# Two weight conversions per unit at the start of a group, four units without one, and three smaller moves, in a fused chunk attention and feed-forward kernel

## The chip, the cores and the metric

The kernel runs on one core of one Trainium2 chip. The metric is device time in microseconds for one execution, the median of three runs before the change.

## What is computed

Attention in chunks of 64 rows over eight heads of width 64, and then a feed-forward layer without a residual:

```python
scores = scale * np.matmul(q_c, k_c.transpose(0, 1, 2, 4, 3))
scores = scores - np.max(scores, axis=-1, keepdims=True)
attn = np.exp(scores)
attn = attn / (np.sum(attn, axis=-1, keepdims=True) + 1e-09)
out = np.matmul(attn, v_c)
...
h = x @ w_in
g = h - np.tanh(h)
return (g @ w_out).astype(np.float32)
```

Here x is the attention's output, 4608 tokens of 512 values, w_in is 512 by 2048 and w_out 2048 by 512, all float32 at the interface.

## The kernel before the change

The 4608 tokens are 36 pairs of 128, in nine groups of four pairs (512 tokens). Each product is made of two halves: a value is split into a high part and the rest, and of the four partial products three are computed.

**Group 0** uses weights as loaded (two float32 tiles, `wh` and `wl`), **group 1** float16 halves of w_in and the float32 halves of w_out, **groups 2 to 8** (class `Fast`) float16 throughout, with sums of w_out blocks that spare one multiplication in eight. While group 0 runs, the attention of groups 0 and 1 (class `Early`, pairs 0 to 7) runs too. While group 1 runs, the weights are converted for it and for what follows, and the attention of group 2 (class `Late`) runs.

**A unit** is one block of 128 columns of w_in. A group has 16 units, in group 1 in the order of `ORDER`; below u0 to u15. For each unit, `FeedForward.written` does in this order: `split` of the unit before (ScalarE rounds it to `gh`, VectorE subtracts to `gl`), the extra steps filed in `at` under 2s-0.5, `gemm1` (12 matmuls into one of two PSUM tiles `ph`), `shrink` (ScalarE tanh into `t`, VectorE h minus tanh), the steps under 2s, `gemm2` of an earlier unit (12 matmuls), and the steps under 2s+1. Every engine takes its instructions in the order in which they are written. So `gemm1` of unit s needs the `ph` of unit s-2 to be free, which in group 1 is after that unit's `gl` (line 554).

**A conversion** (`Half.convert`, lines 448 to 458; below c0 to c15, one per unit, needed by that unit's `gemm1`) is two ScalarE instructions (lines 454 and 455: the two float16 parts) and two of VectorE (457: what the first rounding left; 458: add it to the second part). c(i) writes its parts over the low half of the unit before in `ORDER` (`convert(i)`, line 971), and the same memory is where c(i-1) keeps the intermediate of its line 457, read last by its line 458. So the first ScalarE instruction of c(i) may start only after line 458 of c(i-1). c0, c1 and c2 are made at the end of group 0, c3 to c15 are filed in `at`, c(i) in unit i-3.

**The group's scales.** `ahead` files the steps of `Late`: `greatest` (VectorE makes the scales `to` and `exp` in unit 3, from a maximum that goes out to memory and back), `split` of q, k and v (ScalarE 340, VectorE 341), scores, softmax, transposes, values. `power_of` is six VectorE instructions over one column.

**Pair 6.** `PLAN` is the written order of group 0. Its token `n6` sums pair 6's exponents and divides by the sums head by head, eight ScalarE instructions (line 235). `N` does it with one VectorE instruction (line 237).

Of the kernel before, what the change touches and what calls it, by code (L numbers as in the profile page):

```python
# [18 lines left out]
ALU = mybir.AluOpType  # L19
# [4 lines left out]
H = 8  # L24
# [7 lines left out]
FC = DFF // P  # L32
# [6 lines left out]
FAST = 2  # L39
FAST_LAG = 2  # L40
AHEAD = 3
RAW = 3
WS = 2
EARLY_FC = 8
# [5 lines left out]
ORDER = tuple(i // 2 + i % 2 * FC // 2 for i in range(FC))  # L50

PLAN = """
l0.0 A0 A1 l1.0 v0 v1 a2 a3 l0.1 v2 v3 l1.1 l2.0 l2.1 a4 a5 l3.0 l3.1 F15 x0.0 b0.0 i0.0 z0.0 W0.0 S0 S1 q0 x1.0 m0 p0 e1 P1 F13 S2 N0 T0 b1.0 i1.0 S3 N1 x0.1 z1.0 W1.0 T1 F2 m2 p2 e3 U2 V0 F3 G0.0 D2 P3.0 P3.1 b0.1 U3 D3 i0.1 t T2 x1.1 b1.1 G1.0 t T3 s i1.1 z0.1 W0.1 F2 V2 s z1.1 W1.1 H Y G0.1 x2 G1.1 b2 t s i2 t x3 z2.0 w2.0 s z2.1 w2.1 H h S4 S5 b3 i3 | l4.0 l4.1 v4 v5 z3.0 w3.0 z3.1 w3.1 M4 g2 h l5.0 l5.1 c4 M5 g3 h N4 N5 T4 T5 V4 a6 a7 l6.0 l6.1 c5 S6 S7 v6 v7 g4 h E6 l7.0 l7.1 c6 g5 h M7 l8.0 l8.1 c7 g6 h n6 N7 T6 T7 V6 Z c8 g7 h l9.0 l9.1 c9 g8 h l10.0 l10.1 c10 g9 h l11.0 l11.1 c11 g10 h X l12.0 l12.1 c12 g11 h l13.0 l13.1 c13 g12 h l14.0 l14.1 c14 g13 h l15.0 l15.1 c15 g14 h g15 h h
"""

@with_exitstack
def attn_ffn_kernel(ctx: ExitStack, tc: tile.TileContext, qE, kE, vE, qL, kL, vL, w_in, w_out, out):
# [8 lines left out]
    nc = tc.nc  # L66
# [20 lines left out]
    def place_of(a, part, fc, dtype=F16):  # L87

        return w_pool[fc].tile([P, DM], F32R, name=f"w{a}{part}{fc}").bitcast(dtype)
# [6 lines left out]
    def new_x():  # L96
        return tuple(xpool.tile([P, KC, MOST], F32R, name=f"x{a}") for a in "hl")

    def new_half_x():

        t = xpool.tile([P, KC, MOST], F32R, name="xh").bitcast(F16)
        return t[:, :, :MOST], t[:, :, MOST:]
# [17 lines left out]
    def load_weights(pool, fc, part):  # L120
        if part == 0:
            raws[fc] = pool.tile([P, 2, DM, 2], U32, name="raw", bufs=RAW)
        nc.sync.dma_start(out=raws[fc][:, part], in_=(w_in, w_out)[part][fc])
# [284 lines left out]
    class Half:  # L408
# [39 lines left out]
        def convert(self, fc, place):  # L448


            half_w[fc] = place.rearrange("p (a n) -> p a n", a=2)
            (h, l), (h16, l16), to = wt[fc][0], (half_w[fc][:, i] for i in range(2)), self.to[:, 0:1]
            h, l = h.bitcast(F32), l.bitcast(F32)
            nc.scalar.activation(h16, h, AF.Copy, scale=to)
            nc.scalar.activation(l16, l, AF.Copy, scale=to)
            rest = place_of("l", 0, fc)[:, :DM]
            nc.vector.scalar_tensor_tensor(out=rest, in0=h, scalar=to, in1=h16, op0=ALU.mult, op1=ALU.subtract)  # L457
            nc.vector.tensor_add(l16, l16, rest)
# [57 lines left out]
    class FeedForward:  # L516
# [21 lines left out]
        def shrink(self):  # L538
            fc, t0, t1, n, ph = self.ph
            t = ffn.tile([P, MOST], F32, name="t", bufs=3)[:, :n]  # L540
            if self.g:
                nc.scalar.activation(t, ph, AF.Tanh, scale=self.sig)
                nc.vector.scalar_tensor_tensor(out=ph, in0=ph, scalar=self.sig, in1=t, op0=ALU.mult, op1=ALU.subtract)  # L543
            else:
                nc.scalar.activation(t, ph, AF.Tanh)
                nc.vector.tensor_sub(t, ph, t)
            self.ready = fc, t0, t1, n, ph if self.g else t

        def split(self):
            fc, t0, t1, n, t = self.ready  # L550
# [214 lines left out]
    def ahead(att, at, g):  # L765

        o = 2 * FC * (g - FAST)

        def put(unit, part, f, *args):
            at[o + 2 * unit + part].append(lambda: f(*args))  # L770

        late = g == FAST
        later = g == FAST + 1
        put(1 + later, 0, sums, att, g, "q")
        if not late:
            put(2 + later, 0, sums, att, g, "k")
            put(0 if later else -3, later, att.halves, g, 0)
            put(2, not later, att.halves, g, 1)
        put(1 if late else 4, late, att.sent, g)
        put(2 if late else 4, not late, att.returned, g)  # L780
        put(3 if late else 5, 1, att.greatest, g)
        put(9, 1, lambda: powers.update({g: half.power_of(g)}))
        put(6, 0, lambda: xs.update({g: new_half_x()}))
        for b, u in enumerate((3, 13) if late else (6, 14)):
            put(u, 1, att.split, g, b, "q")
            put(u + 1, 0, att.split, g, b, "k")
            other = u + 2 if late and b else u + 1
            put(other, 1, att.split, g, b, "v")
            if g + 1 < NG:
                for i in (2 * b, 2 * b + 1):  # L790
                    put(u + 1, 1, att.load, FIRST[g + 1] + i, i, "qk")
                    put(other, 1, att.load, FIRST[g + 1] + i, i, "v")
            u += late
            put(u + 2, 0, att.scores, g, b)
            put(u + 2, 1, att.shifted, g, b)
            put(u + 3, 0, att.exponent, g, b)
            put(u + 3, 1, att.totals, g, b)
            put(u + 4, 0, att.divided, g, b)
            put(u + 4 + (not (late and b)), late and b, att.transpose, g, b)
            at[o + 2 * u + 17 - late].insert(0, lambda b=b: att.values(g, b, xs[g]))  # L800
# [4 lines left out]
    x, x1 = new_x(), xpool.tile([P, KC, MOST], F32R, name="xl").bitcast(F32)  # L805
# [13 lines left out]
    att = Early(pool, [psum, ps_a], 4)  # L819
# [28 lines left out]
    def step(token):  # L848
# [53 lines left out]
        elif kind == "q":  # L902
            square(n, 0, junk)
        elif kind == "z":
            high(n, part)
        elif kind in "wW":
            low(n, part, nc.gpsimd if kind == "W" else None)
        elif kind in "Gg":
            gemm1(n, part)
            if kind == "g":  # L910
                shrink()
                split()
        elif kind == "t":
            shrink()
        elif kind == "s":
            split()
        elif kind == "H":
            ff.gemm2((((0, 0),), ((1, 0),), ((0, 1),)))
        elif kind == "h":
            ff.gemm2()  # L920
        elif kind == "Y":
            first_psum.close()
            att.psum = [ps_a]
            ps_o2 = ctx.enter_context(tc.tile_pool(name="ps_o2", bufs=1, space=PSUM, reuse_waits="tile"))
            ff.room(ps_o2, range(2, 4))
            pools.append(ps_o2)
        elif kind == "Z":
            first.close()
            late = ctx.enter_context(tc.tile_pool(name="late_weights", bufs=1, reuse_waits="tile"))
            weight_tiles(late, range(EARLY_FC, FC))  # L930
# [18 lines left out]
    late = ctx.enter_context(tc.tile_pool(name="att", bufs=1, side="right", reuse_waits="tile"))  # L949
    w_pool.update((fc, late) for fc in SPARE)  # L950
    att, half = Late(late), Half(late)
# [4 lines left out]
    xs, powers, at, made = {}, {}, defaultdict(list), {}  # L956
# [13 lines left out]
    def convert(i):  # L970
        half.convert(ORDER[i], place_of("l", 0, ORDER[i - 1]) if i else first_place)

    for i in range(AHEAD, FC):
        at[2 * (i - AHEAD) - 0.5].append(lambda i=i: convert(i))
    at[6].append(for_attention)
    for g in range(FAST, NG):
        ahead(att, at, g)
# [19 lines left out]
    with tc.manual_schedule():  # L997
        half.most(0)
        half.powers(0)
        half.scale_of_sum()  # L1000
        for i in range(AHEAD):
            convert(i)
# [67 lines left out]
```

## Time and profile before

| what | us |
|---|---|
| median of 3 runs | 796.07 (795.02 to 796.33) |
| the profiled execution, device time | 794.97 |
| its span, first to last instruction | 793.2 |
| TensorE busy | 781.5 (99%) |
| VectorE busy | 630.7 (80%) |
| ScalarE busy | 466.8 (59%) |
| GpSimd busy | 407.9 (51%) |

The span is shorter than the device time of the same execution by 1.8 us, which lie around it. Busy times of different engines overlap. All times in the rows further below are in us from the start of the span. Line numbers are those of the kernel before; in the changed kernel the same statements stand one or two lines lower.

### The profile page before, as it was taken

To read this page: it belongs to the slowest core of one execution; us is meant where nothing else is said; L and a number is where in the kernel's file an instruction comes from. 1 tells how busy PE (TensorE), PEld (TensorE's weight loads), DVE (VectorE), ACT (ScalarE), POOL (GpSimd) and SP (SyncE) were. 2 spreads that over 40 slices of the span, in tenths; PEclk is the share of its full clock that TensorE was granted. 3 is DMA by queue.
4 is the path that set the end of the run, shared out by engine and by line. 5 is a ranking of instruction groups with operands and counts; after the bars stand their busy time and mean duration, and the time that the engine had idled before them with its cause. 6 is when DMAs were issued, how large, how long until landed. Compare 5 with 4: busy or idle time off the path is not lost.

```text
span 793.2 us, 21231 instructions
## 1 busy us (share of the span) xinstructions
PE 781.5 (99%) x9096; PEld 659.0 (83%) x9099; DVE 630.7 (80%) x856; ACT 466.8 (59%) x714; POOL 407.9 (51%) x461
## 2 busy tenths in 40 slices
PE   8999999999999999999999999999999999999997
PEld 4877885656788888888888888888888888888887
DVE  5897987999799887877878687968796878687554
ACT  6888996766486446545654474546454655454332
POOL 1100003477786656564656556656656465656463
PEclk9999999999999999999999999999999999999999
DMA  9854442210232322231313123222322230302000
GB/s 355 323 181 156 156 160 63 81 25 8 77 91 81 55 81 55 61 84 34 89 42 97 35 89 57 69 55 81 65 81 55 82 64 2 55 2 54 2 27 27
DMA packets 61054, 64.62 MB, mean 81 GB/s; under 512 B 33952, under 2 KB 42016, under 8 KB 60960
## 3 DMA queue, kind: packets, MB, share of 16 engines
q1 hardware_dynamic: 60528, 62.61, 27.3%
q8 instruction: 71, 1.16, 0.6%
q10 hardware_dynamic: 432, 0.66, 0.2%
q14 instruction: 23, 0.19, 0.1%
HBM read 46.47 MB, written 9.45 MB: 70 GB/s over the span
## 4 chain that ended last, share of the span: by engine, by line
PE 86%; DVE 7%; ACT 4%; issue 1%; DMA 0%; POOL 0%; POOLq 0%; ACTq 0%; DVEq 0%; SPq 0%
PE ph L616 37%; PE po L656 31%; PE po L564 6%; PE ph L534 6%; PE psa L352 3%; DVE wl L457 1%; PE po L731 1%; DVE ph L543 1%; PE ph L863 1%; DVE gl L554 1%; ACT s L217 1%; ACT gh L553 1%; PE psa L182 1%; DVE wh L503 1%; ACT w L132 0%
## 5 line engine op out<-in xcount | busy, mean ns | idle before, releaser
L616 PE MATMUL ph<-xh,wl 128*128 128x256 f16 x2520 | 291.1, 273 | 0.0
L616 PEld LDWEIGHTS <-wl 128*128 128x128 f16 x2520 | 245.4, 98 | 29.3 <-issue 0.5
L625 POOL TENSOR_TENSOR xl<-xl 128x256 f32<-128x256 f32 x111 | 111.8, 1008 | 222.6 <-DVE xl L624 222.0
L623 ACT ACTIVATE t<-ph,sig 128x512 f32<-128x512 f32 x112 | 77.0, 687 | 216.2 <-PE ph L616 214.6
L624 DVE SCALAR_TENSOR_TENSOR xl<-ph,sig,t 128x512 f32<-128x512 f32 x112 | 83.5, 745 | 78.7 <-ACT t L623 78.6
L656 PEld LDWEIGHTS <-wh 128*128 128x128 f16 x1134 | 110.9, 98 | 12.9
L627 POOL TENSOR_TENSOR xl<-xl 128x256 f32<-128x256 f32 x111 | 103.9, 936 | 0.0
L626 POOL TENSOR_TENSOR xl<-xl 128x128 f32<-128x128 f32 x111 | 102.2, 921 | 0.0
L656 PE MATMUL po<-wl,wh 128*128 128x256 f16 x648 | 101.0, 273 | 0.0
L637 DVE SCALAR_TENSOR_TENSOR gl<-xl,to_g,gh 128x896 f16<-128x896 f32 x56 | 83.4, 1489 | 8.0 <-ACT gh L636 8.0
L656 PE MATMUL po<-wh,wh 128*128 128x256 f16 x486 | 85.5, 273 | 0.0
L637 DVE SCALAR_TENSOR_TENSOR wh<-xl,to_g,wh 128x896 f16<-128x896 f32 x56 | 71.1, 1269 | 16.6 <-ACT wh L636 14.8
L656 PEld LDWEIGHTS <-gh 128*128 128x128 f16 x756 | 73.0, 98 | 8.8
L636 ACT ACTIVATE wh<-xl,to_g 128x896 f16<-128x896 f32 x56 | 57.9, 1035 | 32.4 <-POOL xl L627 31.5
L534 PE MATMUL ph<-xh,wl 128*128 128x512 f16 (+2 forms) x252 | 59.5, 376 | 2.5 <-DVE gl L554 2.4
L656 PE MATMUL po<-wh,gh 128*128 128x256 f16 x380 | 61.5, 273 | 0.0
L656 PE MATMUL po<-wl,gh 128*128 128x256 f16 x376 | 58.7, 273 | 0.0
L636 ACT ACTIVATE gh<-xl,to_g 128x896 f16<-128x896 f32 x56 | 57.8, 1032 | 1.3 <-DVE from L114 0.6
L564 PE MATMUL po<-wh,gh 128*128 128x512 f32 x128 | 52.8, 415 | 0.0
L564 PE MATMUL po<-wl,gh 128*128 128x512 f32 x128 | 50.1, 394 | 0.2 <-POOL wl L147 0.2
L656 PEld LDWEIGHTS <-gl 128*128 128x128 f16 x378 | 37.0, 98 | 4.3
L656 PE MATMUL po<-wh,gl 128*128 128x256 f16 x190 | 39.2, 273 | 0.0
(176 smaller groups left out, 1245.7 us busy)
## 6 DMA issues: line engine op xcount, KB each, us to landing
raw<-w_in SPq DMA_DIRECT2D x16, 512.0 KB, 4.0
raw<-w_out SPq DMA_DIRECT2D x16, 512.0 KB, 5.5
xl<-qL SPq DMA_DIRECT2D x28, 256.0 KB, 3.0
rawk<-kL SPq DMA_DIRECT2D x28, 256.0 KB, 3.3
rawv<-vL SPq DMA_DIRECT2D x28, 256.0 KB, 3.4
out<-wh SPq DMA_DIRECT2D x55, 128.0 KB, 1.8
q<-qE SPq DMA_DIRECT2D x8, 256.0 KB, 5.9
v<-vE SPq DMA_DIRECT2D x8, 256.0 KB, 6.1
```

What stands on the lines that cost most here:

```text
L352: nc.tensor.matmul(ps(c, e, hp)[u * D:(u + 1) * D], lhsT=stationary(a, r, e, hp, u), rhs=moving(b, r, e, hp, u), start=first, stop=(i == 2 ...
L534: nc.tensor.matmul(ph, lhsT=w[:, kc * P:(kc + 1) * P], rhs=x[b][:, kc, cols], start=(k == 0), stop=(k == 3 * KC - 1))
L564: nc.tensor.matmul(self.po[t], lhsT=gg[a][:, ts], rhs=wt[fc][1][b], start=(fc == 0 and a == b == 0), stop=(fc == FC - 1 and a == 1))
L616: nc.tensor.matmul(self.ph[:, 1 - f::2, :], lhsT=half_w[fc][:, w, kc * P:(kc + 1) * P], rhs=rhs, start=(k == 0), stop=(k == 3 * KC - 1))
L623: nc.scalar.activation(t, self.ph, AF.Tanh, scale=sig)
L624: nc.vector.scalar_tensor_tensor(out=u[:, :4], in0=self.ph, scalar=sig, in1=t, op0=ALU.mult, op1=ALU.subtract)
L625: engine.tensor_add(u[:, 4:6], u[:, 1:3], u[:, 0:4:3])
L626: engine.tensor_add(u[:, 6], u[:, 1], u[:, 2])
L627: engine.tensor_sub(u[:, 0:4:3], u[:, 0:2], u[:, 2:4])
L636: nc.scalar.activation(gh, u, AF.Copy, scale=powers[1])
L637: nc.vector.scalar_tensor_tensor(out=gl, in0=u, scalar=powers[1], in1=gh, op0=ALU.mult, op1=ALU.subtract)
L656: nc.tensor.matmul(place[m], lhsT=part[:, self.SUM[m]], rhs=w[m][:, o], start=first, stop=(last and part is gl), skip_group_check=True)
```

## The change

In `PLAN`, the token `n6` becomes `N6` (the line is long and otherwise the same). The rest:

```diff
@@ -39,6 +39,7 @@
+CONVERTED = (0, 0, 1, 1, 2, 2, 3, 5, 6, 7, 11, 12, 13)
...
@@ -538,13 +539,14 @@
         def shrink(self):
             fc, t0, t1, n, ph = self.ph
             t = ffn.tile([P, MOST], F32, name="t", bufs=3)[:, :n]
+            u = ph if self.g and fc else t
             if self.g:
                 nc.scalar.activation(t, ph, AF.Tanh, scale=self.sig)
-                nc.vector.scalar_tensor_tensor(out=ph, in0=ph, scalar=self.sig, in1=t, op0=ALU.mult, op1=ALU.subtract)
+                nc.vector.scalar_tensor_tensor(out=u, in0=ph, scalar=self.sig, in1=t, op0=ALU.mult, op1=ALU.subtract)
             else:
                 nc.scalar.activation(t, ph, AF.Tanh)
-                nc.vector.tensor_sub(t, ph, t)
-            self.ready = fc, t0, t1, n, ph if self.g else t
+                nc.vector.tensor_sub(u, ph, t)
+            self.ready = fc, t0, t1, n, u
...
@@ -779,10 +781,10 @@
-        put(9, 1, lambda: powers.update({g: half.power_of(g)}))
+        put(14 if late else 9, 1, lambda: powers.update({g: half.power_of(g)}))
         put(6, 0, lambda: xs.update({g: new_half_x()}))
         for b, u in enumerate((3, 13) if late else (6, 14)):
-            put(u, 1, att.split, g, b, "q")
+            put(u + late, -0.5 if late else 1, att.split, g, b, "q")
...
@@ -970,8 +972,8 @@
-    for i in range(AHEAD, FC):
-        at[2 * (i - AHEAD) - 0.5].append(lambda i=i: convert(i))
+    for i, slot in enumerate(CONVERTED, AHEAD):
+        at[2 * slot - 0.5].append(lambda i=i: convert(i))
```

Conversions c3 to c15 stood one in each of units 0 to 12. They now stand two each in units 0, 1 and 2 (c3 to c8), one each in units 3, 5, 6, 7, 11, 12 and 13, and none in units 4, 8, 9 and 10. `late` is true for the third group (group 2) alone: its `power_of` goes from unit 9 to unit 14, and its two q splits go from behind units 3 and 13 to the start of units 4 and 14, behind the `split` there. In unit 0 of group 1 (fc is 0) VectorE writes h minus tanh to `t` instead of back to `ph`.

ScalarE's instructions from the last rounding `gh` of group 0 on, before the change. Lines 454 and 455 are a conversion, 588 copies the finished sums of group 0, 542 is the tanh of a unit of group 1:

```order
L553 CAST gh<-t 128x512
L454 ACTIVATE wl_1550<-wh_74,to_w 128x512
L455 ACTIVATE wl_1550<-wl_75,to_w 128x512
L588 COPY a<-po_113 128x512
L588 COPY aT<-po_514 128x512
L454 ACTIVATE wl_1580<-wh_1031,to_w 128x512
L455 ACTIVATE wl_1580<-wl_1032,to_w 128x512
L542 ACTIVATE t<-ph,small_105 128x512
L553 CAST gh<-ph 128x512
L454 ACTIVATE wl_1606<-wh_78,to_w 128x512
L455 ACTIVATE wl_1606<-wl_79,to_w 128x512
L542 ACTIVATE t<-ph,small_105 128x512
```

and after it:

```order
L555 CAST gh<-t 128x512
L455 ACTIVATE wl_1537<-wh_1020,to_w 128x512
L456 ACTIVATE wl_1537<-wl_1021,to_w 128x512
L455 ACTIVATE wl_1543<-wh_74,to_w 128x512
L456 ACTIVATE wl_1543<-wl_75,to_w 128x512
L590 COPY a<-po_113 128x512
L590 COPY aT<-po_514 128x512
L455 ACTIVATE wl_1573<-wh_1024,to_w 128x512
L456 ACTIVATE wl_1573<-wl_1025,to_w 128x512
L455 ACTIVATE wl_1579<-wh_78,to_w 128x512
L456 ACTIVATE wl_1579<-wl_79,to_w 128x512
L544 ACTIVATE t<-ph,small_105 128x512
```

Before, one conversion stands before the copies, one behind them ahead of u0's tanh, and one ahead of u1's tanh. After, c1 and c2 stand before the copies (c1 has come from ahead of this `gh`), and c3 and c4 both ahead of u0's tanh.

VectorE's instructions from c3 on, before (457 and 458 a conversion, 543 h minus tanh of a unit, 554 its `gl`):

```order
L457 SCALAR_TENSOR_TENSOR wl_1583<-wh_1031,to_w,wl_1580 128x512
L458 TENSOR_TENSOR wl_1580<-wl_1580,wl_1583 128x512
L543 SCALAR_TENSOR_TENSOR ph<-ph,small_105,t 128x512
L554 TENSOR_TENSOR gl<-ph,gh 128x512
L457 SCALAR_TENSOR_TENSOR wl_1609<-wh_78,to_w,wl_1606 128x512
L458 TENSOR_TENSOR wl_1606<-wl_1606,wl_1609 128x512
L543 SCALAR_TENSOR_TENSOR ph<-ph,small_105,t 128x512
```

and after it:

```order
L458 SCALAR_TENSOR_TENSOR wl_1576<-wh_1024,to_w,wl_1573 128x512
L459 TENSOR_TENSOR wl_1573<-wl_1573,wl_1576 128x512
L458 SCALAR_TENSOR_TENSOR wl_1582<-wh_78,to_w,wl_1579 128x512
L459 TENSOR_TENSOR wl_1579<-wl_1579,wl_1582 128x512
L545 SCALAR_TENSOR_TENSOR t<-ph,small_105,t 128x512
L556 TENSOR_TENSOR gl<-t,gh 128x512
L458 SCALAR_TENSOR_TENSOR wl_1608<-wh_1028,to_w,wl_1605 128x512
L459 TENSOR_TENSOR wl_1605<-wl_1605,wl_1608 128x512
L458 SCALAR_TENSOR_TENSOR wl_1614<-wh_82,to_w,wl_1611 128x512
L459 TENSOR_TENSOR wl_1611<-wl_1611,wl_1614 128x512
L545 SCALAR_TENSOR_TENSOR ph<-ph,small_105,t 128x512
```

u0's line 543 (545 after the change) now has two conversions ahead of it instead of one, and so has u1's; the output of u0's is `t`.

TensorE's instructions at the transposes of pairs 6 and 7 in group 0, before (243 transposes, 182 multiplies with the values, 534 is `gemm1`):

```order
L243 MATMUL psa<-ident,s 128x128 x3
L534 MATMUL ph<-xh,wh_98 128x512 x2
L243 MATMUL psa<-ident,s 128x128
L534 MATMUL ph<-xh,wh_98 128x512 x2
L534 MATMUL ph<-xh,wl_99 128x512
L243 MATMUL psa<-ident,s 128x128 x4
L182 MATMUL psa<-aT,v 64x64 x8
L534 MATMUL ph<-xh,wl_99 128x512
L182 MATMUL psa<-aT,v 64x64 x24
L534 MATMUL ph<-xh,wl_99 128x512 x2
L534 MATMUL ph<-xl,wh_98 128x512 x4
```

and after it:

```order
L244 MATMUL psa<-ident,s 128x128 x4
L535 MATMUL ph<-xh,wh_98 128x512 x4
L535 MATMUL ph<-xh,wl_99 128x512 x4
L244 MATMUL psa<-ident,s 128x128 x4
L183 MATMUL psa<-aT,v 64x64 x8
L535 MATMUL ph<-xl,wh_98 128x512
L183 MATMUL psa<-aT,v 64x64 x24
L535 MATMUL ph<-xl,wh_98 128x512 x3
L566 MATMUL po_113<-wh_96,gh 128x512
```

The four transposes of pair 6 now stand together, and those of pair 7 stand behind eight matmuls of `gemm1` instead of five.

## Rows read from the trace of the kernel before

**Rows 1.** The page's first line.
```profile
span 793.2 us, 21231 instructions
```

**Rows 2.** Waits of TensorE: waited for, us in total, times, longest us.
```profile
PE ph L534 <- DVE gl L554: 2.4, 4, 0.9
...
PE psa L243 <- ACT s L235: 0.6, 1, 0.6
```

**Rows 3.** Timeline of TensorE in group 0: start us, us, line, tiles, idle before.
```profile
65.28 0.38 PE L243 MATMUL psa<-ident,s 128*128 128x128 f32 x2
...
66.27 0.33 PE L243 MATMUL psa<-ident,s 128*128 128x128 f32 x1 [0.61 <-ACT s L235]
```

**Rows 4.** Timeline of VectorE in the same stretch.
```profile
64.44 0.68 DVE L546 TENSOR_TENSOR t<-ph,t 128x512 f32<-128x512 f32 x1
...
66.84 0.68 DVE L237 TENSOR_TENSOR s<-s,sm 128x512 f32<-128x512 f32 x1
```

**Rows 5.** Timeline of TensorE in group 1, units 2, 3, 4, 5, 9, 10, 11.
```profile
126.74 2.75 PE L534 MATMUL ph<-xh,wl 128*128 128x512 f16 x12 [0.32 <-DVE gl L554]
...
132.09 2.76 PE L534 MATMUL ph<-xh,wl 128*128 128x512 f16 x12
...
137.47 2.76 PE L534 MATMUL ph<-xh,wl 128*128 128x512 f16 x12
...
143.24 2.75 PE L534 MATMUL ph<-xh,wl 128*128 128x512 f16 x12 [0.24 <-DVE gl L554]
...
166.02 2.75 PE L534 MATMUL ph<-xh,wl 128*128 128x512 f16 x12
...
172.39 2.75 PE L534 MATMUL ph<-xh,wl 128*128 128x512 f16 x12 [0.86 <-DVE gl L554]
...
178.84 2.75 PE L534 MATMUL ph<-xh,wl 128*128 128x512 f16 x12 [0.95 <-DVE gl L554]
```

**Rows 6.** Timeline of ScalarE where group 0 ends and group 1 begins.
```profile
117.97 0.61 ACT L553 CAST gh<-t 128x512 fp32r<-128x512 f32 x1
118.48 0.72 ACT L454 ACTIVATE wl<-wh,to_w 128x512 f16<-128x512 f32 x1
119.11 0.71 ACT L455 ACTIVATE wl<-wl,to_w 128x512 f16<-128x512 f32 x1
...
127.66 1.90 ACT L106 ACTIVATE t<-xl 128x2048 uint8<-128x2048 f32 x1
...
129.56 0.58 ACT L553 CAST gh<-ph 128x512 fp32r<-128x512 f32 x1
```

**Rows 7.** Timeline of VectorE in the same stretch.
```profile
119.85 0.75 DVE L457 SCALAR_TENSOR_TENSOR wl<-wh,to_w,wl 128x512 f16<-128x512 f32 x1 [0.54 <-ACT wl L455]
120.64 0.42 DVE L458 TENSOR_TENSOR wl<-wl,wl 128x512 f16<-128x512 f16 x1
121.24 0.69 DVE L586 COPY a<-po 128x512 f32<-128x512 f32 x1 [0.17 <-PE po L564]
...
123.34 0.75 DVE L457 SCALAR_TENSOR_TENSOR wl<-wh,to_w,wl 128x512 f16<-128x512 f32 x1
...
124.58 0.76 DVE L543 SCALAR_TENSOR_TENSOR ph<-ph,small,t 128x512 f32<-128x512 f32 x1
...
130.16 0.69 DVE L554 TENSOR_TENSOR gl<-ph,gh 128x512 fp32r<-128x512 f32 x1 [0.62 <-ACT gh L553]
```

**Rows 8.** Timeline of VectorE in later units of group 1.
```profile
165.89 1.30 DVE L457 SCALAR_TENSOR_TENSOR wl<-wh,to_w,wl 128x512 f16<-128x512 f32 x1
167.22 0.83 DVE L458 TENSOR_TENSOR wl<-wl,wl 128x512 f16<-128x512 f16 x1
...
204.92 0.76 DVE L543 SCALAR_TENSOR_TENSOR ph<-ph,small,t 128x512 f32<-128x512 f32 x1 [2.46 <-ACT t L542]
```

**Rows 9.** Timeline of ScalarE at group 1's unit 3.
```profile
140.12 1.15 ACT L340 ACTIVATE wh<-xl,to 128x1024 f16<-128x1024 f32 x1 [3.61 <-DVE exp L327]
```

**Rows 10.** The window at the end: stretch, length, busy by engine, granted clock, DMA.
```profile
790.00:793.20 3.20, 0.00 (x0) 0.00 (x0) 0.02 (x1) 0.00 (x0) 0.03 (x1) 0.82 0.32 107
```

More of the change, by code (lines that the diff above doesn't have):

```diff
@@ L52 @@
 PLAN = """
-l0.0 A0 A1 l1.0 v0 v1 a2 a3 l0.1 v2 v3 l1.1 l2.0 l2.1 a4 a5 l3.0 l3.1 F15 x0.0 b0.0 i0.0 z0.0 W0.0 S0 S1 q0 x1.0 m0 p0 e1 P1 F13 S2 N0 T0 b1.0 i1.0 S3 N1 x0.1 z1.0 W1.0 T1 F2 m2 p2 e3 U2 V0 F3 G0.0 D2 P3.0 P3.1 b0.1 U3 D3 i0.1 t T2 x1.1 b1.1 G1.0 t T3 s i1.1 z0.1 W0.1 F2 V2 s z1.1 W1.1 H Y G0.1 x2 G1.1 b2 t s i2 t x3 z2.0 w2.0 s z2.1 w2.1 H h S4 S5 b3 i3 | l4.0 l4.1 v4 v5 z3.0 w3.0 z3.1 w3.1 M4 g2 h l5.0 l5.1 c4 M5 g3 h N4 N5 T4 T5 V4 a6 a7 l6.0 l6.1 c5 S6 S7 v6 v7 g4 h E6 l7.0 l7.1 c6 g5 h M7 l8.0 l8.1 c7 g6 h n6 N7 T6 T7 V6 Z c8 g7 h l9.0 l9.1 c9 g8 h l10.0 l10.1 c10 g9 h l11.0 l11.1 c11 g10 h X l12.0 l12.1 c12 g11 h l13.0 l13.1 c13 g12 h l14.0 l14.1 c14 g13 h l15.0 l15.1 c15 g14 h g15 h h
+l0.0 A0 A1 l1.0 v0 v1 a2 a3 l0.1 v2 v3 l1.1 l2.0 l2.1 a4 a5 l3.0 l3.1 F15 x0.0 b0.0 i0.0 z0.0 W0.0 S0 S1 q0 x1.0 m0 p0 e1 P1 F13 S2 N0 T0 b1.0 i1.0 S3 N1 x0.1 z1.0 W1.0 T1 F2 m2 p2 e3 U2 V0 F3 G0.0 D2 P3.0 P3.1 b0.1 U3 D3 i0.1 t T2 x1.1 b1.1 G1.0 t T3 s i1.1 z0.1 W0.1 F2 V2 s z1.1 W1.1 H Y G0.1 x2 G1.1 b2 t s i2 t x3 z2.0 w2.0 s z2.1 w2.1 H h S4 S5 b3 i3 | l4.0 l4.1 v4 v5 z3.0 w3.0 z3.1 w3.1 M4 g2 h l5.0 l5.1 c4 M5 g3 h N4 N5 T4 T5 V4 a6 a7 l6.0 l6.1 c5 S6 S7 v6 v7 g4 h E6 l7.0 l7.1 c6 g5 h M7 l8.0 l8.1 c7 g6 h N6 N7 T6 T7 V6 Z c8 g7 h l9.0 l9.1 c9 g8 h l10.0 l10.1 c10 g9 h l11.0 l11.1 c11 g10 h X l12.0 l12.1 c12 g11 h l13.0 l13.1 c13 g12 h l14.0 l14.1 c14 g13 h l15.0 l15.1 c15 g14 h g15 h h
 """
```

## The prediction

> **What bounds the kernel now.** I read the page first: a span of 793.2 us [rows 1], with TensorE busy for 99% of it, so a change that removes no matmul can win only what TensorE waits. Then TensorE's waits: from the point where the edits act, the list holds little, 2.4 us in four waits for VectorE's `gl` in group 1 and 0.6 us for ScalarE's division of pair 6 [rows 2]. The timelines then show how much air there is around them. Units of group 1 follow each other in 5.38 us when nothing is late (u3 at 132.09, u4 at 137.47 [rows 5]). u2 starts late at 126.74, u5 at 143.24 is 0.39 late, u10 and u11 at 172.39 and 178.84 come 6.37 and 6.45 us after the unit before, 0.99 and 1.07 late [rows 5]. So 2.45 us can be won at u5, u10 and u11. Behind group 1 no wait is listed, so a delay that group 1 leaves reaches the end whole.
>
> **How long one conversion takes.** Rows 6 and 7 have c2 with nothing in its way: ScalarE starts it at 118.48, the second instruction at 119.11 and ends it at 119.82. VectorE's first instruction waits for just that end (its row names ScalarE as the releaser) and starts at 119.85, the second starts at 120.64 and ends at 121.06. That is a lap of 2.58 us, of which ScalarE works 1.34. The next conversion writes over what the last VectorE instruction reads, so of two in a row the second starts 2.61 us behind the first, and ScalarE, which takes its instructions in order, stands idle in between with the tanh queued behind it. A conversion alone in a unit never shows this, since a unit lasts twice as long as a lap.
>
> **Units 0 to 2, step by step** (on the clock of before; the early gain comes off below). ScalarE rounds group 0's last unit at 117.97 and is free at 118.48 [rows 6]. *Before*, c2 takes that place and c3 the next. *After*, c1 does, 118.48 to 121.06, then c2, 121.09 to 123.67. c3's ScalarE part can run from 123.70 to 125.04. But VectorE's copies of group 0's sums and five small instructions stand between c2 and c3, 2.10 us from 121.24 to 123.34 [rows 7]; they start at 123.6 behind c2, so c3's VectorE part starts at 125.7 and ends 1.21 later, at 126.91. Then c4: ScalarE from 126.94, done 128.28, VectorE from 128.31, and u0's subtraction follows a conversion's start by 1.24 (123.34 to 124.58 [rows 7]): 129.55, done at 130.31 against 125.34. Writing to `t` pays here: u2 need no longer wait for u0's `gh` and `gl`. It still starts at about 130.4 instead of 126.74, 3.6 late.
>
> u0's `gh` starts at 130.35 and c5 at 130.86 (0.51 behind, as 117.97 and 118.48 in [rows 6]); c6 starts 2.61 later, u1's tanh 1.23 after that at 134.7 and takes 0.57. The sum over q stands behind it, 1.90 us (127.66 to 129.56 [rows 6]), so u1's `gh` comes at 137.2. From `gh` to the end of `gl` it is 1.29 (129.56 to 130.16 plus 0.69 [rows 6, 7]): 138.46. u3 starts at 138.5 instead of 132.09, 6.4 late.
>
> c7 starts at 137.7, c8 2.61 later, its second VectorE instruction at 142.45; u2's subtraction ends at 143.66, its `gl` at 145.0. u4 starts at 145.05 instead of 137.47: **7.6 late**. From unit 3 on the conversions stand alone again, and u5 follows in 5.38.
>
> **What is given back.** The q split: ScalarE sat 3.61 us before it, waiting for the scales, with u3's `gh` queued behind [rows 9]; behind that `gh`, it frees u5 of its 0.39. Units 8 to 10 lose a conversion each, on VectorE 1.30 and 0.83 here [rows 8], and `power_of` leaves unit 9; that is more than each was late, so u10 and u11 get their 0.99 and 1.07 back. Together 2.45. VectorE now enters that stretch late itself, so I leave 0.3 of new waits there (bounds 0 and 0.8). `power_of` in unit 14 costs nothing: VectorE idles 2.46 us there before its subtraction [rows 8]; without that cover it would cost under 1 us, six small instructions. The q split at unit 14 and c13 to c15 one unit later than before lie in the same loose units: nothing, up to 0.5.
>
> **Pair 6.** TensorE starts its transposes at 65.28 and stands from 65.66 to 66.27 for the third head pair [rows 3]. VectorE's multiplication, 0.68 long, comes behind the subtraction of 64.44 to 65.12 and ends near 65.7 [rows 4], so TensorE waits until 65.75 and then not again. But pair 7's multiplication moves back by the same 0.60, from 66.84 to 67.4, and its transposes behind three more matmuls. Bounds: 0, if pair 7 eats it, and 0.99, the whole way from 65.28 to 66.27. I take 0.4, between the two, since the new order gives TensorE other work until then.
>
> **The sum.** +7.6, -2.45, +0.3, -0.4: **+5.0 us**. The profiled execution would go from 794.97 to 800.0. It was 1.10 below the median of the runs, so for the median I add the same 5.0 to 796.07: 801.1. About 0.2% (1.6 us) is what a measurement of this kernel can tell from no change.
>
> **Rivals.** *Two in a row cost no more than ScalarE's own 1.34 each* (the second does not really wait for the first). Then VectorE reaches its copies near 121.9, and u0's subtraction ends near 126.9. From there 0.5 to c5, 2.5 for two conversions on ScalarE, 0.6 for the tanh, 1.9 for the sum over q and 1.3 to the end of `gl` give 133.7: u3 is 1.6 late, u4 and the rest follow without a wait, and the sum is +1.6 - 2.45 - 0.4 = -1.3, about 795. For it: nothing in the trace shows the wait, since no two stand in a row there. Against it: the memory is the same, so without the wait the result would be another.
>
> *Faster*: the slack of u3 takes up the pairs. It decides at u1's `gl`: if that ends by 132.05, u3 keeps its start, and the change wins 2.45 and 0.4 and u2's 0.3, 3.2 us, 793. Before, it ended at 130.85 [rows 7], 1.2 of air. Two laps and a sum over q must fit into that, so it needs the first rival to hold and more.
>
> *Slower still*: u2 waits 4.0 us (u1's matmuls end 0.32 before 126.74 [rows 5]), longer than any wait of TensorE in this trace. In the last 3.2 us, behind the last matmul, the mean granted clock is 0.82 [rows 10], which at two levels means that it fell to 1.2 GHz on the way. If it falls in this wait, u2 and the 12 matmuls behind it take twice their 5.38; 2.7 us of that lie in u3's own wait, and u4, bound by c7 and c8, absorbs another part: +1.4, 802.5; up to +4 if it stays low through u3. The Trainium skill, "TensorE: Matmul & The Clock Gate", section "Part 1: The HAM clock gate (the "warmup" mystery)", says that the throttled level is the default and that only activity releases it; the last window agrees. By that rule an idle stretch costs again after it ends, which is this rival. The sum by rows does without it, because the clock stood at full speed through every wait seen between matmuls. VectorE's conversions beside GpSimd's sums belong here too: 1.30 and 0.83 instead of 0.75 and 0.42 [rows 7, 8], 0.96 a conversion, up to 1.5 us for the pairs in units 1 and 2.
>
> **How the numbers follow.** The forecast 0.78, with its own range of +3.9 (pair 6 wins all, nothing new waits) to +6.6 (GpSimd in the way of two conversions). Slower still 0.12, no change 0.06, faster 0.04. So slower 0.90, same 0.06, faster 0.04. The range from 798.5 to 804.5 takes in the forecast's own and most of the slower case, and leaves out the other two.
>
> **What would show it.** Right: TensorE's longest wait in group 1 is that of u2, near 4 us, released by VectorE's h minus tanh; u3 waits near 2.7, u4 near 1, both for `gl`; ScalarE idles about 1.2 us between the two conversions of a pair, released by line 458 (459 after the change); waits of u10 and u11 are gone; TensorE's wait at the transposes moves to VectorE. Wrong: no idle time inside a pair on ScalarE, or u3 starting less than 3 us late. I would be wrong by size if u4 to u12 still wait on `gl` (slower), or if VectorE's copies no longer stand between c2 and c3 in time (faster by up to 2).

## The result, and the profile after

The changed kernel takes 800.77 us (median of four runs, 800.69 to 801.16) against 795.55 beside it on the same chip: a ratio of 1.0068, interval 1.0051 to 1.0085. It is slower, by 5.4 us by the ratio and by 5.2 between the two medians. The profiled execution took 800.69 us with a span of 798.9, against 794.97 and 793.2 [rows 1].

Waits of TensorE in the changed kernel, in the form of [rows 2]; `h` minus tanh is line 545 here, `gl` line 556, `gemm1` line 535:

```profile
PE ph L535 <- DVE t L545: 3.9, 1, 3.9
PE ph L535 <- DVE gl L556: 3.0, 2, 1.6
...
PE psa L244 <- DVE sm L229: 0.5, 1, 0.5
```

One long wait on u0's subtraction, two on `gl`, and a short one at pair 6's transposes. The timeline of TensorE says where, for u0's second part, u2 to u5, u10, u11, and the first unit of group 2:

```profile
121.76 2.33 PE L535 MATMUL ph<-xh,first_place 128*128 128x512 f16 x10
...
130.56 4.08 PE L535 MATMUL ph<-xh,wl 128*128 128x512 f16 x12 [3.88 <-DVE t L545]
...
138.82 2.75 PE L535 MATMUL ph<-xh,wl 128*128 128x512 f16 x12 [1.43 <-DVE gl L556]
...
145.87 2.75 PE L535 MATMUL ph<-xh,wl 128*128 128x512 f16 x12 [1.56 <-DVE gl L556]
...
151.21 2.76 PE L535 MATMUL ph<-xh,wl 128*128 128x512 f16 x12
...
179.17 2.76 PE L535 MATMUL ph<-xh,wl 128*128 128x512 f16 x12
184.55 2.76 PE L535 MATMUL ph<-xh,wl 128*128 128x512 f16 x12
...
212.51 1.48 PE L618 MATMUL ph<-xh,first_place 128*128 128x256 f16 x12
```

Before, the part of u0 shown first (its last ten matmuls, below "u0's second part") stood at 121.49, so this execution comes 0.27 late into group 1 for reasons ahead of it. Against [rows 5], with that taken off, u2 is 3.55 us late (130.56 - 126.74 - 0.27), u3 6.46 and u4 8.13. From u5 on no unit waits; u10 is 6.51 late, u11 5.44, group 2's first unit 5.48 (before at 206.76). So 2.65 us come back between u4 and u11, and what is left then reaches the end: from group 2's start to the end of the span it is 586.4 us in both.

ScalarE where group 0 ends and group 1 begins, to be read against [rows 6]; 455 and 456 are a conversion, c1 to c4 and then c7, c8:

```profile
118.71 0.72 ACT L455 ACTIVATE wl<-wh,to_w 128x512 f16<-128x512 f32 x1
119.34 0.71 ACT L456 ACTIVATE wl<-wl,to_w 128x512 f16<-128x512 f32 x1
121.38 0.72 ACT L455 ACTIVATE wl<-wh,to_w 128x512 f16<-128x512 f32 x1 [1.34 <-DVE wl L459]
...
124.06 0.72 ACT L455 ACTIVATE wl<-wh,to_w 128x512 f16<-128x512 f32 x1 [0.39 <-DVE wl L459]
...
127.27 0.72 ACT L455 ACTIVATE wl<-wh,to_w 128x512 f16<-128x512 f32 x1 [1.88 <-DVE wl L459]
...
128.51 0.67 ACT L544 ACTIVATE t<-ph,small 128x512 f32<-128x512 f32 x1
...
137.94 0.72 ACT L455 ACTIVATE wl<-wh,to_w 128x512 f16<-128x512 f32 x1
...
141.17 0.72 ACT L455 ACTIVATE wl<-wh,to_w 128x512 f16<-128x512 f32 x1 [1.89 <-DVE wl L459]
```

Each second conversion of a pair waits for the first one's last VectorE instruction, and u0's tanh at 128.51 stands behind both. c1 and c2 stand in a row too, though by no entry of the table; pair 6's edit below shows why. The distances are 2.67 us (118.71 to 121.38), 3.21 (124.06 to 127.27, where VectorE's copies stood ahead of c3's part) and 3.23 (137.94 to 141.17). VectorE shows why the last is so long; c6, then c7:

```profile
135.10 1.19 DVE L458 SCALAR_TENSOR_TENSOR wl<-wh,to_w,wl 128x512 f16<-128x512 f32 x1 [1.46 <-ACT wl L456]
...
139.31 0.90 DVE L458 SCALAR_TENSOR_TENSOR wl<-wh,to_w,wl 128x512 f16<-128x512 f32 x1 [0.54 <-ACT wl L456]
140.24 0.83 DVE L459 TENSOR_TENSOR wl<-wl,wl 128x512 f16<-128x512 f16 x1
```

Alone these take 0.75 and 0.42 [rows 7]. In the windows of two microseconds the fifth pair of numbers is GpSimd's busy time, and the granted clock, as a share of full speed, comes right behind it:

```profile
128.00:130.00 2.00, 0.00 (x0) 0.00 (x0) 1.33 (x3) 1.17 (x2) 0.00 (x0) 0.97 0.00 0
130.00:132.00 2.00, 1.44 (x4) 0.56 (x4) 1.20 (x2) 1.46 (x3) 0.00 (x0) 0.50 0.00 0
132.00:134.00 2.00, 2.00 (x8) 0.75 (x6) 1.18 (x2) 0.66 (x2) 0.00 (x0) 0.68 0.00 0
134.00:136.00 2.00, 2.00 (x10) 1.54 (x9) 0.90 (x1) 2.00 (x4) 1.43 (x2) 1.00 0.00 0
...
138.00:140.00 2.00, 1.18 (x6) 0.58 (x6) 1.39 (x2) 1.27 (x3) 2.00 (x4) 1.00 0.04 1
```

GpSimd works all of 138 to 140, under c7. And the clock fell to its lower level (0.50 of full speed, 1.2 GHz) in u2's wait, so that u2's 12 matmuls took 4.08 us instead of 2.75. u3 and u4 wait for `gl` behind it, so in this kernel that did not move them.

### The profile page after: what moved, and what is told of

It is laid out like the page before. It is cut to its first block, busy times and chain, and to the rows that moved or that the text cites. A ratio compares the mean times of both kernels' runs of the same rounds, so it can differ in the third digit from the quotient of the medians.

```text
span 798.9 us, 21230 instructions
## 1 busy us (share of the span) xinstructions
PE 782.7 (98%) x9096; PEld 659.0 (82%) x9099; DVE 629.0 (79%) x857; ACT 465.9 (58%) x706; POOL 407.1 (51%) x461
## 4 chain that ended last, share of the span: by engine, by line
PE 89%; DVE 5%; ACT 5%; issue 1%; POOLq 0%; ACTq 0%; POOL 0%
PE ph L618 37%; PE po L658 31%; PE po L566 8%; PE ph L535 7%; PE psa L353 3%; ACT s L218 1%; PE ph L865 1%; PE po L733 1%; DVE wl L148 1%; PE psa L183 1%; DVE wl L458 1%; ACT wl L456 1%; DVE w L141 1%; ACT wl L455 1%; ACT t L107 0%
## 5 line engine op out<-in xcount | busy, mean ns | idle before, releaser
L618 PEld LDWEIGHTS <-wl 128*128 128x128 f16 x2520 | 245.4, 98 | 29.3 <-issue 0.5
L535 PEld LDWEIGHTS <-wl 128*128 128x128 f16 x180 | 17.1, 100 | 29.7 <-issue 12.0
```

The costliest lines, as they stand in the source:

```text
L535: nc.tensor.matmul(ph, lhsT=w[:, kc * P:(kc + 1) * P], rhs=x[b][:, kc, cols], start=(k == 0), stop=(k == 3 * KC - 1))
L618: nc.tensor.matmul(self.ph[:, 1 - f::2, :], lhsT=half_w[fc][:, w, kc * P:(kc + 1) * P], rhs=rhs, start=(k == 0), stop=(k == 3 * KC - 1))
```

## The experiments

Theory: the loss is the lap of a conversion over shared memory, in the pairs. Rivals came up on the way: that the amount of work in the early units does it, that the clock does, that the other edits lose or win. Times are medians, ratios stand against the kernel before on the same chip with a 95% interval, five rounds each.

### The table alone, and everything but the table

```diff
+CONVERTED = (0, 0, 1, 1, 2, 2, 3, 5, 6, 7, 11, 12, 13)
...
-    for i in range(AHEAD, FC):
-        at[2 * (i - AHEAD) - 0.5].append(lambda i=i: convert(i))
+    for i, slot in enumerate(CONVERTED, AHEAD):
+        at[2 * slot - 0.5].append(lambda i=i: convert(i))
```

> The kernel before with the table of conversions alone; `power_of`, the q splits, the output of unit 0 and pair 6 as before. Lap theory (the second of two conversions in a row waits on VectorE's last instruction of the first, ScalarE and the tanh behind it stand): c1 stays in its early place here, so u2 starts near 129.3 on the clock of before, u3 near 136.1 (4.0 late), u4 near 142.7 (5.2 late), u5 6.4 late since the q split still holds u3's `gh`; u10 and u11 get 2.1 back: +4.3 us, 800. Rival, it is the other moves that cost about half of it: +2 to +3 us here.

And the changed kernel with `CONVERTED = tuple(range(13))`:

> The changed kernel with c3 to c15 one per unit in units 0 to 12 as before; the other moves stay, and with them the order c1, c2 in a row behind group 0's last `gh`. Lap theory: one lap alone, so u2 0.7 late, u3 and u4 1.2 late, u5 gets its 0.39 back, u10 and u11 keep a part of their waits since the conversions of units 8 to 10 stay: +0.5 us against the kernel before (-0.5 to +1.2), some 5 us under the changed kernel. Rival, the other moves cost half: +2 to +3.

Measured: the table alone 800.78 us, 1.0065 (1.0052 to 1.0078); all but the table 794.93, 0.9992 (0.9983 to 1.0001). The loss is the table's. The other edits together come out about even (0.6 us faster by the ratio, where I had expected 0.5 slower): u2 waits 1.24 us in that kernel too, for a reason that I found only with pair 6's edit below.

u9, u10 and u11 in the kernel with the table alone:

```profile
173.59 2.76 PE L535 MATMUL ph<-xh,wl 128*128 128x512 f16 x12
...
178.97 2.76 PE L535 MATMUL ph<-xh,wl 128*128 128x512 f16 x12
...
184.34 2.76 PE L535 MATMUL ph<-xh,wl 128*128 128x512 f16 x12
```

and u10 in the kernel with everything but the table:

```profile
173.12 2.75 PE L535 MATMUL ph<-xh,wl 128*128 128x512 f16 x12 [0.85 <-DVE gl L556]
```

So the table by itself frees u10 and u11 (5.38 and 5.37 us from unit to unit), with the q splits and `power_of` where they were. Without the table u10 still comes 6.37 us behind u9 (166.75), as in [rows 5], and only u11 is free.

### A room of its own for the intermediate

```diff
-            rest = place_of("l", 0, fc)[:, :DM]
+            rest = ffn.tile([P, MOST], F32, name="t", bufs=3).bitcast(F16)[:, :DM]
```

in the changed kernel, so that a conversion may start while the one before it still adds. First with the change's table:

> The changed kernel with one thing different: the intermediate of a conversion's first VectorE instruction goes to a tile of the rotating pool of `t` instead of the memory that the next conversion overwrites. Same work on every engine, same table; the second conversion of a pair need not wait for VectorE. Lap theory: ScalarE runs the two in 2.5 us, u3 at most 1.6 late, u4 nearly on time, waits of u5, u10 and u11 gone: 1 to 2 us under the kernel before, 794 (793 to 796). Rival, it is the amount of work in units 0 to 2 and not the wait: unchanged, near 800.5.

Measured: 795.72 us, 1.0001 (0.9993 to 1.0010). ScalarE in this kernel, c3 and c4:

```profile
123.23 0.73 ACT L455 ACTIVATE wl<-wh,to_w 128x512 f16<-128x512 f32 x1
123.85 0.72 ACT L456 ACTIVATE wl<-wl,to_w 128x512 f16<-128x512 f32 x1
124.61 0.72 ACT L455 ACTIVATE wl<-wh,to_w 128x512 f16<-128x512 f32 x1
125.24 0.70 ACT L456 ACTIVATE wl<-wl,to_w 128x512 f16<-128x512 f32 x1
```

No idle time is left in the pair: 1.38 us from start to start instead of 3.21. This takes back 5.1 us of the loss, but not the 6 to 7 that I expected: u2, u3 and u4 still wait 0.53, 1.42 and 0.67 us. The 5.1 include the lap of c1 and c2, which now stand ahead of group 0's last tanh (114.27 and 115.63). Two tables with fewer pairs tell whether that is the work itself. One pair alone, `CONVERTED = (0, 1, 2, 3, 3, 4, 5, 6, 7, 11, 12, 13, 14)`, with the room:

> As the one before, with the table (0, 1, 2, 3, 3, 4, 5, 6, 7, 11, 12, 13, 14): one conversion in each of units 0 to 2 as before, two in unit 3 where ScalarE stood 3.61 us idle, none in units 8, 9 and 10. Lap theory: u2, u3 and u4 on time, waits of u5, u10 and u11 gone: 2.5 to 3 us under the kernel before, 793. Rival (amount of work): two conversions in unit 3 make u5 late by 1 to 2 us, so -0.5 to -1.5, 794.5.

and without it:

> The changed kernel with the table (0, 1, 2, 3, 3, 4, 5, 6, 7, 11, 12, 13, 14) of the 792.85 us run, but with the intermediate where it was, in the memory that the next conversion overwrites. Lap theory: the laps of c1, c2 (1.1 us) and of the pair in unit 3 (0 to 1.5 us) come back: 794.7 (793.8 to 795.5). Rival, the gain was the table's alone: 792.9.

and the room with one conversion in each unit, `tuple(range(13))`:

> The changed kernel with own room for the intermediate and one conversion per unit in units 0 to 12. Lap theory: nothing late before u9, since c1 and c2 no longer wait for one another, but units 8 to 10 keep their conversions, so u10 and u11 wait again, 1 to 2 us: 794.0 to 794.5. Rival, the room alone is the gain: 792.9.

Measured: 792.85 us (0.9967, 0.9954 to 0.9979) with the room and one pair; 797.00 (1.0014, 1.0006 to 1.0023) with one pair and the old room; 792.77 (0.9965, 0.9952 to 0.9977) with the room and no pair. So with the room, one pair in unit 3 costs nothing and three pairs in units 0 to 2 cost 2.95 us (795.72 - 792.77): that is work that the early units can't take. At u4 a part of it is c7 and c8 beside GpSimd's sums, where line 458 takes 1.30 and 1.21 us. Two expectations were missed. One pair in the old room lost 1.1 by the ratio (1.5 between the medians) where I expected a small gain, since u2 waits 1.20 us there as in the kernel without the table, and behind the pair in unit 3 u5 and u6 wait 0.97 and 0.66 us. And with one conversion in each unit u10 and u11 do not wait at all, though I had expected them to: I had taken the conversions of units 8 to 10 for the one cause.

### The room in the kernel before

```diff
-            rest = place_of("l", 0, fc)[:, :DM]
+            rest = ffn.tile([P, MOST], F32, name="t", bufs=3).bitcast(F16)[:, :DM]
```

> The kernel before with one change: the intermediate of a conversion lies in a tile of its own (the ring of the tanh's output), no more in the memory that the next conversion writes. Everything else stays, also the old place of the q split and of the powers. My reading: the waits of u10 and u11 came from VectorE queueing behind the conversions, and the room takes them away without any other edit; u5's 0.39 stays, since the q split still waits for the scales behind unit 3. Expected 793.4 (0.9973), with u10 and u11 not waiting and u5 waiting 0.2 to 0.5 us. Rival: the waits of u10 and u11 go only because the powers left unit 9; then they stay here and the time is 795.0 to 795.5 (ratio 0.999 to 1.000).

Measured: 794.27 us, 0.9986 (0.9977 to 0.9994), between the two. From u1 to group 2 it is 80.83 us (124.75 to 205.58) instead of 83.10, so the waits of u5, u10 and u11 go by the room alone; u2 still waits 0.46. But u1 starts at 124.75 instead of 123.66. Of that, 0.72 stood already at group 0's last `gemm1` (113.39 against 112.67), for a reason that I don't know; in the other profiled executions this place lies between 112.57 and 114.07. The other 0.37 come behind it, where c1 and c2, free to move, now stand ahead of group 0's last tanh on ScalarE.

### One pair, in unit 0

The changed kernel with `CONVERTED = (0, 0, 1, 2, 3, 4, 5, 6, 7, 8, 9, 10, 11)`:

> The changed kernel with the table (0, 0, 1, 2, 3, 4, 5, 6, 7, 8, 9, 10, 11): one pair, in unit 0, the old room, one conversion in each unit to 11. Lap theory, dose for dose: by the same walk as for three pairs u2 is 3.6 late and u3 3.8 (138.5 became 135.9), instead of 7.6 at u4; less what u5 and the others give back, +1.5 to +2.5 against the kernel before: 797.7. Rival, what costs is the three units together or the missing conversions later: within 1 us of the run with one conversion per unit (794.9).

Measured: 797.89 us, 1.0029 (1.0020 to 1.0038), the time that I expected. Its waits of TensorE show one line for group 1:

```profile
PE ph L535 <- DVE t L545: 3.9, 1, 3.9
```

u2's wait is there whole, and no wait behind it. But the way to this time is not the one that I expected. u2 and u3, and u1's `gl`, for which u3 waits in the change:

```profile
131.59 4.44 PE L535 MATMUL ph<-xh,wl 128*128 128x512 f16 x12 [3.91 <-DVE t L545]
...
138.61 2.76 PE L535 MATMUL ph<-xh,wl 128*128 128x512 f16 x12
...
136.39 0.69 DVE L556 TENSOR_TENSOR gl<-ph,gh 128x512 fp32r<-128x512 f32 x1 [0.61 <-ACT gh L555]
```

The granted clock fell behind u2's wait here too (0.59 and 0.56 from 132 to 136). u1's `gl` is done at 137.08, so u3 could have started at 137.13, as it follows `gl` by 0.05 in the change. It starts at 138.61, 7.02 us behind u2, because TensorE itself was late: **here the clock costs 1.48 us**. So u3 comes 5.25 late instead of the 3.8 that I expected, and 2.6 us come back behind it. That the sum met the forecast is luck. The change loses 2.9 us more than this kernel (800.77 - 797.89). As the clock costs nothing in the change, the pairs of units 1 and 2 are worth more than that, by these figures about 4.4 us.

### The clock kept up

Sixteen matmuls whose result nobody reads, between u1 and u2 of the changed kernel:

```diff
+    def idle():
+        ps = ps_a.tile([P, 2, 2, 4, CH], F32, name="psa")
+        out = ps[:, 0].rearrange("p a b k -> p (a b k)")
+        for _ in range(16):
+            nc.tensor.matmul(out, lhsT=half_w[ORDER[1]][:, 0, :P], rhs=nx[0][:, 0, :], start=True, stop=True)
+
+    at[3].append(idle)
```

> The changed kernel with 16 extra matmuls into the unused `psa` tile between u1 and u2 (their result is used by nobody), 3.5 us of work in the 3.9 us that TensorE stands before u2, so that the granted clock does not fall there. In the changed kernel it was 0.50 from 130 to 132 and u2's twelve matmuls took 4.08 instead of 2.75. Lap theory: u3 waits for u1's `gl` anyway, so the fall costs nothing: 800.8, within 0.3. Rival, the clock is a part of the loss: 1.2 to 1.5 us less, 799.4.

Measured: 801.42 us, 1.0070 (1.0056 to 1.0083), as the change without them. u2 and u3 in this kernel:

```profile
131.19 2.75 PE L535 MATMUL ph<-xh,wl 128*128 128x512 f16 x12 [0.46 <-DVE t L545]
...
139.41 4.44 PE L535 MATMUL ph<-xh,wl 128*128 128x512 f16 x12 [2.73 <-DVE gl L556]
```

u2 runs at full speed now, and u3 comes no earlier: 17.05 us behind u0's second part (122.36) instead of 17.06 (138.82 - 121.76). The slow matmuls of the change lay inside u3's own wait, which is 2.73 where it was 1.43. The clock then falls at the end of that wait instead, and u3's matmuls take 4.44 us. u4, and u2's `gl`, for which it waits in the change:

```profile
146.44 2.76 PE L535 MATMUL ph<-xh,wl 128*128 128x512 f16 x12
...
145.16 0.69 DVE L556 TENSOR_TENSOR gl<-ph,gh 128x512 fp32r<-128x512 f32 x1 [0.71 <-ACT gh L555]
```

u2's `gl` is done at 145.85, and u4 starts 0.59 behind it where it takes 0.06 in the change: the later fall costs about 0.5 us. The equal totals therefore don't show that the clock is free; u3's start does, for the change. The total is equal because c7 runs clear of GpSimd here and takes 0.75 and 0.42 us on VectorE again, so that u2's `gl` starts 22.80 us behind u0's second part instead of 23.36, 0.56 earlier. The two together bring u4 24.08 us behind u0's second part, against 24.11 in the change.

### Pair 6 alone, and the change without it

The kernel before with one token of `PLAN` changed:

```diff
-... c7 g6 h n6 N7 T6 T7 V6 ...
+... c7 g6 h N6 N7 T6 T7 V6 ...
```

> The kernel before with one change: the token for pair 6 in group 0's written order (its normalisation is one VectorE instruction instead of eight of ScalarE). The prediction priced it at -0.4 (0 to -0.99). The changed kernel's trace shows 0.13 us won at the transposes. So theory one: 795.4, ratio 0.9995 to 1.000. Theory two: freeing ScalarE in group 0 lets the order of c1 and c2 move together at the end of group 0, as in the kernel with everything but the table, where u2 waited 1.24 us; then u2 waits about 1 us and the time is 796.0 to 796.4 (1.0005 to 1.001).

Measured: 797.39 us, 1.0024 (1.0015 to 1.0033): **this edit alone loses 1.9 us**. At the transposes it does what it should: TensorE goes from the start of its last four matmuls ahead of them to the first `gemm2` matmul behind in 7.29 us (64.59 to 71.88) instead of 7.48 (64.37 to 71.85). The loss stands 50 us later. ScalarE in this kernel, at the end of group 0, c1 and c2:

```profile
118.53 0.72 ACT L454 ACTIVATE wl<-wh,to_w 128x512 f16<-128x512 f32 x1
119.16 0.71 ACT L455 ACTIVATE wl<-wl,to_w 128x512 f16<-128x512 f32 x1
121.20 0.72 ACT L454 ACTIVATE wl<-wh,to_w 128x512 f16<-128x512 f32 x1 [1.34 <-DVE wl L458]
```

and TensorE's u2, which stood at 126.74 with a wait of 0.32 [rows 5]:

```profile
129.04 2.75 PE L534 MATMUL ph<-xh,wl 128*128 128x512 f16 x12 [2.59 <-DVE gl L554]
```

With eight instructions of ScalarE gone, c1 falls behind the last rounding of group 0, in a row with c2, and pays a lap. Before, it stood ahead of group 0's last tanh, at 113.85. The section on the kernel before says that every engine takes its instructions in the written order. At the end of group 0 that is not so: no edit touches c1's place in the text, and still it moved. The order there is settled when the kernel is built. The loss is larger than either theory gave, since u2 in this kernel still waits for u0's `gl`: 2.59 us, against 1.24 in the kernel with everything but the table, where u0's `t` lets it go at the subtraction. Two more kernels test this. First the changed kernel with `n6` and with one conversion in each unit, so that u0's `t`, the later q split and the later powers are left:

> The changed kernel without two of its edits: one conversion per unit again, and pair 6 divided head by head as before. What is left of the change: u0's output to its own tile, the later q split and the later powers. Everything but the table gave 0.9992, pair 6's edit alone 1.0024, and pair 6's edit brings the conversions c1 and c2 together at the end of group 0. If that is where its cost lies, then here c1 and c2 stand apart, u2 does not wait (its wait of 1.24 us goes), u5 and one of u10 and u11 are won, and the time is near 793.9 (0.9978 to 0.9985). Rival: pair 6's cost lies in group 0 itself; then u2 still waits near 1.2 us here.

Then the changed kernel with `n6` alone taken back:

> The changed kernel with one edit taken back: pair 6 is divided head by head as before. The table of two conversions per unit stays. If pair 6's edit costs a lap through the order of c1 and c2, that lap is one of the two ahead of u0's subtraction: u2 then starts about 1.2 us earlier, and as u3 and u4 are bound by the pairs of units 1 and 2 behind it, all of it arrives: 799.3 to 799.6 (1.0046 to 1.0052). The change would then be a loss of about 3.8 from the table and 1.2 from pair 6. Rival: the pairs of units 1 and 2 are the bound whatever c1 does, as the table alone gave 800.8: then 800.8, ratio 1.0065.

Measured: 793.05 us, 0.9971 (0.9960 to 0.9983), and 799.06, 1.0048 (1.0034 to 1.0062). In the first, u2 runs on behind u1 without a wait, and in all of group 1 one wait is left:

```profile
124.64 5.34 PE L535 MATMUL ph<-xh,wl 128*128 128x512 f16 x24
...
171.66 2.75 PE L535 MATMUL ph<-xh,wl 128*128 128x512 f16 x12 [0.23 <-DVE gl L556]
```

From u0's second part to group 2 it is 82.60 us instead of 85.27. It wins more than expected, since here u10 and u11 come nearly free without the table (5.76 and 5.50 us behind the unit before). Why u10 does not in the kernel with everything but the table was not told apart. In the second u2 waits less and u3 more (u2, then u3):

```profile
129.35 2.75 PE L535 MATMUL ph<-xh,wl 128*128 128x512 f16 x12 [1.53 <-DVE t L545]
137.79 4.39 PE L535 MATMUL ph<-xh,wl 128*128 128x512 f16 x12 [2.92 <-DVE gl L556]
```

**What the parts are worth.** In ratios to the kernel before, one edit at a time: the two smaller moves with u0's `t` 0.9971; the table on top of them 1.0048, that is +0.77% or 6.1 us; pair 6 on top of both 1.0068, +0.20% or 1.6 us. So +5.4 = -2.3 + 6.1 + 1.6. With the room the table costs 0.36% (1.0001 against 0.9965), 2.9 us: about half of its cost is laps, half is work that comes too early into units 0 to 2. Differences of ratios carry both intervals, so each of the last two terms is good to about 1.5 us or a little more, and pair 6's 1.6 is not clear of noise by the times alone. Its own kernel (1.0015 to 1.0033) is, and so are the traces: from u0's second part to group 2 it is 82.60 us, then 88.54 with the table, then 90.75 with pair 6 as well, against 85.27 before. In these terms are the clock's 0.5 us in the kernel with `n6` taken back and GpSimd's 0.56 in the change. The versions without the table, with the room (792.77) or with `n6` (793.05), beat both kernels.

## Why the prediction came out, step by step

The time was right, 801.1 for 800.77, and the terms of units 0 to 4 nearly so; the sum was right in part by a term credited to the wrong edit, and in part by luck. The base of 796.07 was 0.52 above the median beside the change, and the sum of +5.0 was 0.2 below the difference of the medians (5.22) and 0.7 below that of the profiled executions (5.72); the two errors run against each other.

**The lap** is as worked out: idle time of 1.34 us between the conversions of an undisturbed pair, 2.67 from start to start where I had 2.61. That u0's subtraction falls behind both laps and the copies gave u2 3.6 late; measured 3.55. u3: 6.4, measured 6.46.

**u4** was 7.6, measured 8.13. The step that fell short is the one from c7 to c8, 2.61 us by an undisturbed lap: c7's VectorE part took 0.90 and 0.83 beside GpSimd instead of 0.75 and 0.42, 0.56 more. I had this as part of a rival and not in the sum. The kernel with the clock kept up shows that this reaches u2's `gl`: without GpSimd beside c7 it comes 0.56 earlier. c6's 1.19 cost nothing: the sum over q on ScalarE ended behind it anyway.

**Given back**: 2.45 forecast, 2.65 measured; of the 0.3 for new waits nothing came. The 0.2 are about what the forecast left out at u9, which follows u8 in 5.61 us before (160.41 to 166.02). I credited u10 and u11 to the conversions that leave units 8 to 10 and to `power_of`. That the conversions suffice the kernel with the table alone shows. That they are not the only way the kernel with `n6` and no table shows, which wins 2.67 us in group 1, 2.17 of them behind u4, and the kernel with the room alone. So the same waits can be won without the table's price. Being late is at least not enough: with pair 6's edit alone the units come 2.3 us late, and u10 and u11 still wait 0.87 and 0.94. Whether the q split or the powers matter for u10 and u11 was not told apart.

**Pair 6** is the step that failed: -0.4, "between the two" bounds. At its place it won 0.13 (7.35 us instead of 7.48, 64.71 to 72.06): TensorE still waits 0.47 us, now for VectorE's reciprocal of the sums (line 229). As a whole the edit costs 1.6 to 1.9 by the times, through c1. I had seen c1 move, and its lap stands in the 3.6 of u2, but as the table's: the order shown ahead of the prediction belongs to all edits together, and I took no part of it back for pair 6. The total was not hurt by this. Who had kept pair 6's edit on the strength of that -0.4 would have lost by it.

**The range.** By its own terms the lower end of the forecast's own range is +4.2 (7.6 - 2.45 - 0.99) and not +3.9; nothing hangs on it.

**The rivals.** That two in a row cost only ScalarE's time is refuted by the idle 1.34 us. The faster case fell with it. The slower case happened in its mechanism and not in its price: the clock fell in u2's wait, as that rival said, and u3 waits 1.43 instead of 2.7 because TensorE itself came late, but u3's start is bound by `gl` and did not move, which the kernel with the clock kept up shows (17.05 us behind u0's second part against 17.06). The Trainium skill, "TensorE: Matmul & The Clock Gate", section "Part 1: The HAM clock gate (the "warmup" mystery)", says that the throttled level is the default and activity releases it; the windows agree (0.97, then 0.50 and 0.68 with TensorE at work again, then 1.00). That it costs time follows only where nothing else is late. With one pair in unit 0 nothing else was, and 1.48 us were paid. In the change without pair 6's edit the clock fell in u3's wait instead; u2's `gl` was done at 144.22 and u4 started at 144.78, so about 0.5 us were paid there.

## What to carry to other kernels

Before two steps that stood apart are put in a row, look for memory that the second writes and the first still reads: a lap that was free in a loop of one per unit becomes idle time of an in-order engine, with everything queued behind it. A scratch tile of its own removes the lap, but not the cost of work that comes early into units with no air. An edit that frees an engine can move other work to a worse place far behind it when the kernel is built, so it should be measured alone, and its price read at the places where the order moved, not only where the edit stands. When TensorE slows down behind a wait, look at what the next unit waits for before counting the loss: the same fall of the clock cost nothing where that came later still, and 1.48 us where it was already there.

## What I had not expected of the hardware

TensorE's granted clock fell to 0.50 of full speed in or right at the end of waits of 3.91 us (one pair in unit 0), 3.88 (the change), 2.92 (the change without pair 6's edit), 2.88 (the table alone) and 2.73 us (with the filler matmuls), and it cost 1.48 us in the first, nothing in the change, and about 0.5 in the third and the last; with the table alone u4's own wait took it up. VectorE's conversion, which takes 0.75 and 0.42 us alone, takes up to 1.19 and 0.83 beside GpSimd's sums in the change, and up to 1.30 and 0.83 in the kernel before [rows 8]. With the change's table that was worth 0.5 us at u4.
